# The product of attention and V moves on PE from the end of a step to its start, directly behind the scores

## The chip, the cores and the metric

The kernel runs on one core of a Trainium2 chip. The metric is device time in microseconds of the whole program, the median of several runs. A profiled execution has a time of its own, which is given beside the runs.

Engines are named as the profile names them: PE multiplies matrices (PEld is its weight load), DVE works on vectors, ACT applies functions and copies, POOL works on vectors too, SP issues most DMAs. Each engine runs its instructions in the order of the program and waits at semaphores for the others.

## The reference, cut to what matters

```python
# q, k, v: (8, 8, 576, 64); w_in (512, 1024), conv_w (3, 1024), w_out (1024, 512)
scores = q @ k.T / 8
kth = np.partition(scores, -32, axis=-1)[..., -32:-31]      # 32nd largest of each row
scores = np.where(scores >= kth, scores, -1e9)
attn = softmax(scores)
x = (attn @ v)                                              # heads side by side: (8, 576, 512)
h = np.maximum(x @ w_in, 0)
conv = conv_w[0] * h[s-1] + conv_w[1] * h[s] + conv_w[2] * h[s+1]
out = (h * sigmoid(conv)) @ w_out
```

So for each of 64 heads: scores of 576 by 576, the 32nd largest of each row as a threshold, a softmax over what reaches it, the product with v. Then, for each of 8 batches, a gated feed-forward network over 576 rows. All of it is in 32-bit floats.

## The kernel before, in words

**Tiles.** Two heads are worked on together (a pair of heads, `pc`). A tile (`t`) is 128 rows of scores by 576 keys; two tiles, `h` = 0 and `h` = 1, make a unit. There are 288 tiles, so 144 units. Where the last 64 rows of the heads are worked on, one unit serves two products of 64 columns (`single`); otherwise a unit has one product of 128 columns (`st`).

**The loop.** `iteration(it)` issues one step for all engines. Several tiles are under way, each at another stage: in step `it` the scores of tile `it + 3` are computed (L233, for both tiles of a unit at once, in the step of the first), tile `it + 2` is copied from PSUM (`evacuate`, L243), `it` and `it - 1` go through DVE's search for the largest values, `it - 2` gets its signs (`sides`, L295), `it - 3` its exponential (`expo`, L305), `it - 4` its select and its weighing (`select` L314, `weigh` L319; this gives `e`), and `it - 5` is transposed by PE (`transposes`, L335) and copied by ACT (`transposed`, L344). Between these the feed-forward network of an earlier batch is worked on as filler: `run_units` issues matmuls of `Expand` (L451) and `Contract` (L608) by a credit that grows by a fixed amount in each step (`FEED`, `LEAN`, `EARLY`).

**Two kinds of step.** The tile whose scores come next has `h` = 0 in every second step; this step is called `crowded` in the code, and here step A. In step A the tile transposed has `h` = 0 as well, and the scores of a whole unit stand at the step's end. In the other step, B, the transposed tile has `h` = 1, and behind the filler PE issues the transposes of the reciprocals of the sums (`norms`, L395, in some steps), of the tails (the 64 keys beyond 512 of both tiles, `tails`, L353), the edges of the next scores (`edge_product`, L221 and L225), and the product with v (`av`, L374 and L377).

**The product.** When a unit's second tile has been transposed, its products are put into `av_next` with `st.at = it + 1`. The next step is crowded, so the condition keeps them, and they are issued one step later, in step B, as the last thing on PE. Their result is copied in the step after that by `av_out` (L384).

**PSUM.** One bank, `mixed`, holds the edges, the tails' transpose and the two results of products, 128 columns each. Another tile of two banks, `weights_ps`, holds the exponential, the tanh of the filler, and constants that `select` reads. Accesses of different engines to one bank are put in the order of the program by semaphores, also where they go to different columns.

**Orders.** PE, ACT, DVE and POOL take their instructions in the order in which the code issues them, in all steps of the main loop; behind it, for the rest of the filler, the order comes from the framework's scheduler. ACT's order in a step is: copies of finished filler, `sides`, `evacuate`, `transposed`, `tailed`, `av_out`, later `expo`, `edges`, `tanh`, and the copy of the reciprocals in `norms`, which goes on by DMA to the rows that POOL normalises with (`normalise`, L419 to L421).

Of the kernel before, what the change touches and what calls it, by code (L numbers as in the profile page):

```python
# [71 lines left out]
def attend_and_feed(ctx: ExitStack, tc: tile.TileContext, q, k, v, weights, out, shared, finish=None):  # L72
# [155 lines left out]
    def scores(t):  # L228
        if t.h:
            return  # L230
        if not t.edged:
            edge_product(t)
        for one in (t, t.mate) if t.single else (t,):  # L233
            kx, qx, at = one.pc.nat["k"], one.pc.nat["q"], one.st.c
            for h in range(2):
                d, keys = slice(h * D, (h + 1) * D), slice(h * TAIL, h * TAIL + MAIN)
                if t.single:
                    r = slice(half_of(one, h) * D, (half_of(one, h) + 1) * D)
                    nc.tensor.matmul(s_ps[one.h][r], lhsT=qx[d, at:at + TAIL], rhs=kx[d, keys], start=True, stop=True)
                else:  # L240
                    nc.tensor.matmul(s_ps[h], lhsT=qx[d, at:at + P], rhs=kx[d, keys], start=True, stop=True)  # L241

    def evacuate(t):  # L243
        t.row = rows[:, t.n % XBUFS]
        x = t.x = t.row[:, 8:S + 8]
        at = TAIL if t.h else 0
        nc.scalar.copy(out=x[:, at:at + MAIN], in_=s_ps[t.h])  # L247
        if t.h == 0:
            r = t.n % XBUFS
            if r + 1 < XBUFS:  # L250
                first, step = r * (S + 16) + 8 + MAIN, S + 16 - MAIN
                ends = flat[:, first:first + 2 * step].rearrange("p (h c) -> p h c", h=2)[:, :, 0:TAIL]
                nc.scalar.copy(out=ends, in_=edge_ps.rearrange("p (h c) -> p h c", h=2))
            else:
                nc.scalar.copy(out=x[:, MAIN:S], in_=edge_ps[:, 0:TAIL])
                nc.scalar.copy(out=rows[:, 0, 8:8 + TAIL], in_=edge_ps[:, TAIL:2 * TAIL])
# [78 lines left out]
    def transposes(t):  # L335
        if t.h == 0:
            t.unit.pT = att.tile([P, 2, NI, P], F32, name="pT", bufs=PTB)
            t.unit.pTt = att.tile([P, P], F32, name="pTt", bufs=PTB)
        o = TAIL if t.h else 0
        tp = t.tp = bank("pt")  # L340
        for i in range(NI):
            nc.tensor.transpose(tp[:, i * P:(i + 1) * P], t.e[:, o + i * P:o + (i + 1) * P], ident)  # L342

    def transposed(t):  # L344
        pT, tp = t.unit.pT, t.tp
        if t.single:
            nc.scalar.copy(out=pT[:, :, :, t.h * TAIL:(t.h + 1) * TAIL].rearrange("p h i c -> p i h c"),
                           in_=tp.rearrange("p (i h c) -> p i h c", i=NI, h=2))
        else:
            nc.scalar.copy(out=pT[:, t.h], in_=tp.rearrange("p (i c) -> p i c", i=NI))  # L350
# [15 lines left out]
    def av(st):  # L366
        state.avs += 1
        a = st.a = x_ps[state.avs % 2]
        c = slice(st.off, st.off + st.w)
        for i in range(NI + 1):  # L370
            for h in range(2):
                r = slice(h * D, (h + 1) * D)
                if i < NI:
                    nc.tensor.matmul(a[r, 0:st.w], lhsT=st.pc.vn[:, h, i], rhs=st.unit.pT[:, st.half[h], i, c],  # L374
                                     start=(i == 0), stop=False)
                else:
                    nc.tensor.matmul(a[r, 0:st.w], lhsT=st.pc.vt[:, h], rhs=st.unit.pTt[:, c],  # L377
                                     start=False, stop=True)

    def av_out(st):  # L380
        pc = st.pc
        if st.c == 0:
            pc.xt = att.tile([P, pc.c1 - pc.c0], F32, name=f"xt{pc.part}", bufs=3 + pc.part)
        nc.scalar.copy(out=pc.xt[:, st.c:st.c + st.w], in_=st.a[:, 0:st.w])  # L384
# [312 lines left out]
    for b in range(B):  # L697
        for part, blocks in enumerate(PARTS):
            for g in range(NPAIR):
# [3 lines left out]
                for i in blocks:  # L703
                    st = Box()
# [88 lines left out]
    av_next, out_next, rec_next, norm_wait, tail_next = [], [], [], [], []  # L793

    def iteration(it):
# [4 lines left out]
        tX, tD, tE = tiles.get(it - 3), tiles.get(it - 4), tiles.get(it - 5)  # L800
# [5 lines left out]
        while split_next() and it > NT + 4:  # L806
            pass
        crowded = n < NT and work[n].h == 0
        avs = [st for st in av_next if not crowded or it > st.at]
        av_next = [st for st in av_next if st not in avs]  # L810
        both = tE is not None and tE.h == 1
        if tE is not None:
            transposes(tE)
        if n < NT:
# [7 lines left out]
            sides(tC)  # L822
        if pre is not None:
            evacuate(pre)
        if tE is not None:
            transposed(tE)
        while tail_next:
            tailed(tail_next.pop())
        outs, out_next = out_next, []
        for st in outs:  # L830
            av_out(st)
            if st.final and st.pc.g % 2:
                norm_wait.append((it + NORM_LAG, st.pc))

        if exact:
            a_ops, b_ops = [], list(exact_ops(tB)) if tB is not None else []
# [56 lines left out]
            edge_product(work[n + 1])  # L893
        if n < NT:
            scores(tiles[n])
        for st in avs:
            av(st)
        if tE is not None and tE.k == 0:
            load_v(tE.pc)
        out_next.extend(avs)  # L900
# [21 lines left out]
    with tc.manual_schedule(engines=engines) if engines else nullcontext():  # L922
        fetch(pcs[0])
        state.fetched = 1
        load_blocks(W_FIRST)
        for it in range(-3, NT + 6):
            iteration(it)
    if finish is not None:
        finish(edge_ps[0:1, 0:1])
    while expands or contracts or any(x.waiting for x in lanes) or pool_tasks or tanh_next or tanh_now or gates:  # L930
        it += 1
        iteration(it)
# [127 lines left out]
```

## Time and profile before

| | us |
|---|---|
| median of 3 runs | 1108.52 |
| lowest and highest run | 1107.27 to 1109.16 |
| profiled execution, its own time | 1109.58 |
| span of its instructions | 1107.7 |

The granted clock of PE was 0.98 of full speed over the span and 1.00 from 200 to 1000 us. The profile's page gives busy times; a wait is the idle time of an engine before an instruction, with what ended it. The chain that ended last is followed back from the last instruction: at each step to what released it, or else to the instruction before it on the same engine. A row of the timeline has start, duration, engine, line of the code, operation, tiles and shapes, and in brackets the idle time before it with what ended it; a row of the chain has start, duration, engine, tile, line.

### The profile page before, as it was taken

The numbers are of one execution on the slowest core, as the hardware profiler recorded it, in microseconds if no ns is written. First come the engines' busy times: TensorE is split into PE (matmuls) and PEld (weight loads), VectorE is DVE, ScalarE is ACT, GpSimd is POOL, SyncE is SP. The second block draws the span as 40 slices with busy tenths as digits, with TensorE's granted clock in tenths as the row PEclk, the third lists the DMA queues.
The fourth block names the chain that finished last, engine by engine and source line by source line (L and its number), as shares of the span: only waits on it lengthen the run. The fifth ranks groups of instructions, "written<-read, shape, count | busy, mean of one in ns | idle before, by whom it ended". The sixth has DMA issues, their size and how long they took to land.

```text
span 1107.7 us, 27589 instructions
## 1 busy us (share of the span) xinstructions
PE 1021.4 (92%) x7890; PEld 762.3 (69%) x7890; DVE 1038.6 (94%) x5792; ACT 958.7 (87%) x2417; POOL 935.2 (84%) x1224
## 2 busy tenths in 40 slices
PE   6776788899999999999999999999999999998996
PEld 2443466676777777776777767776777767776985
DVE  8999999999999999999999999999999999999670
ACT  7888889989999998989999998999999998999551
POOL 6778779799989989899988989899988989899610
PEclk9979899999999999999999999999999999999998
DMA  8232212223311322212311322222311322221101
GB/s 297 88 117 65 76 53 64 68 66 96 93 45 58 118 64 72 88 57 91 107 43 48 127 66 62 81 71 92 89 62 49 99 93 63 70 62 47 37 20 42
DMA packets 71154, 85.95 MB, mean 78 GB/s; under 512 B 12848, under 2 KB 45904, under 8 KB 70992
## 3 DMA queue, kind: packets, MB, share of 16 engines
q1 hardware_dynamic: 70992, 84.09, 24.2%
q8 instruction: 65, 1.06, 0.4%
q14 instruction: 97, 0.79, 0.2%
HBM read 74.47 MB, written 9.58 MB: 76 GB/s over the span
## 4 chain that ended last, share of the span: by engine, by line
PE 55%; DVE 33%; ACT 9%; issue 1%; DMA 1%; POOL 0%; SPq 0%; ACTq 0%; POOLq 0%
PE mc L608 13%; PE me L451 12%; DVE cand L263 9%; PE pt L342 8%; PE mixed L374 8%; DVE e L330 7%; PE s L241 7%; DVE z L312 5%; DVE cand L285 3%; ACT weights_ps L309 2%; ACT side L297 2%; DVE g L520 2%; DVE rows L283 2%; PE mixed L377 2%; DVE scratch L161 2%; PE weights_ps L608 2%
## 5 line engine op out<-in xcount | busy, mean ns | idle before, releaser
L263 DVE MAX8 cand<-rows 128x8 f32<-128x82 f32 (+1 forms) x2016 | 480.6, 240 | 0.0
L302 POOL TENSOR_TENSOR z<-rows,side 128x579 f32<-128x579 f32 x288 | 347.7, 1207 | 72.0 <-ACT side L297 70.7
L309 ACT ACTIVATE weights_ps<-rows,z 128x576 f32<-128x576 f32 x288 | 220.0, 764 | 23.5 <-DVE e L330 8.2
L330 DVE SCALAR_TENSOR_TENSOR e<-rows,kth,weights_ps 128x576 f32<-128x576 f32 x288 | 231.5, 804 | 0.6 <-DVE cand L263 0.3
L451 PE MATMUL me<-x_hi,wi 128*128 128x258 f32 (+1 forms) x952 | 228.0, 310 | 0.0
L342 PEld LDWEIGHTS pt<-ident,e 128*128 128x128 f32 x1152 | 124.3, 144 | 146.3 <-issue 25.2
L297 ACT ACTIVATE side<-rows 128x576 bf16<-128x576 f32 x288 | 223.6, 776 | 0.0
L312 DVE MAX8 z<-z 128x8 f32<-128x576 f32 x288 | 213.8, 742 | 0.0
L342 PE MATMUL pt<-ident,e 128*128 128x128 f32 x1152 | 193.6, 292 | 12.3 <-DVE e L330 10.9
L608 PE MATMUL mc<-wo,split 128*128 128x512 f32 x732 | 200.0, 404 | 0.0
L350 ACT COPY pT<-pt 128x512 f32<-128x512 f32 x256 | 152.9, 597 | 42.0 <-PE pt L342 41.2
L247 ACT COPY rows<-s 128x512 f32<-128x512 f32 x288 | 166.8, 579 | 6.6 <-PE s L241 4.9
L241 PE MATMUL s<-k,q 64*128 64x512 f32 x512 | 166.2, 665 | 4.5 <-ACT rows L247 4.1
L374 PE MATMUL mixed<-pT,vn 128*64 128x128 f32 (+1 forms) x2560 | 168.3, 277 | 0.0
L451 PEld LDWEIGHTS me<-x_hi,wi 128*128 128x128 f32 x952 | 162.3, 190 | 0.2 <-ACT g L465 0.2
L374 PEld LDWEIGHTS mixed<-pT,vn 128*64 128x64 f32 x2560 | 133.4, 142 | 17.5 <-issue 1.4
L608 PEld LDWEIGHTS mc<-wo,split 128*128 128x128 f32 x732 | 128.5, 189 | 20.5
L451 PE MATMUL me<-x_lo,wi 128*128 128x258 f32 (+1 forms) x476 | 142.2, 299 | 0.0
L484 POOL TENSOR_SCALAR t<-g,cr 128x256 f32<-128x256 f32 (+1 forms) x228 | 116.5, 511 | 0.0
L283 DVE MAX8 rows<-cand 128x8 f32<-128x21 f32 x576 | 106.0, 184 | 0.0
L498 POOL TENSOR_TENSOR t<-t,t 128x256 f32<-128x256 f32 (+1 forms) x114 | 91.3, 801 | 9.5
L451 PEld LDWEIGHTS me<-x_lo,wi 128*128 128x128 f32 x476 | 91.1, 191 | 0.0
(126 smaller groups left out, 1703.0 us busy)
## 6 DMA issues: line engine op xcount, KB each, us to landing
vn<-in_v_main_dram SPq DMA_DIRECT2D x64, 256.0 KB
k<-in_k_dram SPq DMA_DIRECT2D x32, 384.0 KB
k<-in_k_dram SPq DMA_DIRECT2D x32, 352.0 KB
out_dram<-o SPq DMA_DIRECT2D x26, 256.0 KB
q<-in_q_dram SPq DMA_DIRECT2D x32, 192.0 KB
rb<-row SPq DMA_DIRECT2D x64, 96.0 KB
q<-in_q_dram SPq DMA_DIRECT2D x32, 160.0 KB
raw<-in_w_in_dram SPq DMA_DIRECT2D x16, 256.0 KB
```

What stands on the lines that cost most here:

```text
L241: nc.tensor.matmul(s_ps[h], lhsT=qx[d, at:at + P], rhs=kx[d, keys], start=True, stop=True)
L247: nc.scalar.copy(out=x[:, at:at + MAIN], in_=s_ps[t.h])
L263: yield lambda c=c, at=at, n=n: nc.vector.max(out=t.cand[:, c:8 * CHUNKS:CHUNKS], in_=t.x[:, at:at + n])
L297: nc.scalar.activation(out=t.side[:, 2:S + 2], in_=t.x, func=AF.Sign, scale=-OVER, bias=t.row[:, 7:8], accum_out=t.cnt)
L302: nc.gpsimd.tensor_tensor(t.z[:, 8:S + 11], t.row[:, 6:S + 9], t.side, ALU.mult)
L309: nc.scalar.activation(out=e_ps, in_=t.x, func=AF.Exp, scale=scale, bias=t.shift)
L312: nc.vector.max(out=t.z[:, 0:8], in_=t.z[:, 10:S + 10])
L330: nc.vector.scalar_tensor_tensor(out=t.e, in0=t.x, scalar=kth[:, t.n:t.n + 1], in1=e_ps, op0=ALU.is_ge, op1=ALU.mult, accum_out=t.pc.sums[ ...
L342: nc.tensor.transpose(tp[:, i * P:(i + 1) * P], t.e[:, o + i * P:o + (i + 1) * P], ident)
L374: nc.tensor.matmul(a[r, 0:st.w], lhsT=st.pc.vn[:, h, i], rhs=st.unit.pT[:, st.half[h], i, c], start=(i == 0), stop=False)
L451: nc.tensor.matmul(mm[:, 0:w], lhsT=wt, rhs=xx, start=(n == 0), stop=(n == len(ops) - 1))
L608: nc.tensor.matmul(mm[0:m], lhsT=x[:, i], rhs=wo[:, e, f], start=start, stop=stop)
```

## The change

The product is issued at the start of step B, ahead of the transposes, and no longer at its end; its condition now keeps it for one step in every case. On PE it thus stands directly behind the scores, which end step A. On ACT the copy of the transposes, `transposed`, comes behind the copies of tails and of the product before, no longer ahead of them. Filler and its credit are as they were.

```diff
         crowded = n < NT and work[n].h == 0
-        avs = [st for st in av_next if not crowded or it > st.at]
+        avs = [st for st in av_next if it > st.at]
         av_next = [st for st in av_next if st not in avs]
         both = tE is not None and tE.h == 1
+        for st in avs:
+            av(st)
         if tE is not None:
             transposes(tE)
...
         if pre is not None:
             evacuate(pre)
-        if tE is not None:
-            transposed(tE)
         while tail_next:
             tailed(tail_next.pop())
         outs, out_next = out_next, []
...
                 norm_wait.append((it + NORM_LAG, st.pc))
+        if tE is not None:
+            transposed(tE)
...
         if n < NT:
             scores(tiles[n])
-        for st in avs:
-            av(st)
         if tE is not None and tE.k == 0:
             load_v(tE.pc)
         out_next.extend(avs)
```

## Rows read from the trace of the kernel before

**Rows 1.** The page: the chain that ended last by engine; and busy time of each engine from 200 to 1000 us (stretch, length, then busy us with the number of instructions for PE, PEld, DVE, ACT and POOL, granted clock, DMA share, GB/s).

```profile
PE 55%; DVE 33%; ACT 9%; issue 1%; DMA 1%; POOL 0%; SPq 0%; ACTq 0%; POOLq 0%
...
200.00:1000.00 800.00, 777.47 (x6245) 585.63 (x6245) 779.44 (x4497) 733.33 (x1855) 735.23 (x948) 1.00 0.24 75
```

**Rows 2.** The waits of the whole span: who waited for whom, us in total, times, longest us.

```profile
ACT pT L350 <- PE pt L342: 41.2, 52, 2.2
PE mixed L353 <- ACT rows L253: 34.1, 34, 1.7
...
DVE hot L316 <- ACT weights_ps L512: 15.9, 38, 0.7
...
PE s L395 <- ACT rows L247: 13.4, 14, 1.9
...
ACT rT L397 <- PE s L395: 5.0, 11, 0.8
```

**Rows 3.** The chain that ended last: the first of seven places where it leaves PE at the reciprocals' transpose (its copy on ACT), one of them in full length from 744 to 752 us, and the last.

```profile
244.68 0.26 ACT rT L397
...
744.27 1.06 PE s L241 x4
745.33 0.59 PE pt L342 x4
...
747.78 0.12 PE s L395
...
747.92 0.03 ACT rT L397
...
750.12 0.57 ACT pT L350
...
750.85 0.16 ACT xt L384
...
751.68 0.54 ACT weights_ps L512
...
752.25 0.24 DVE hot L316 x2
...
999.57 0.03 ACT rT L397
```

**Rows 4.** The timeline of PE at the end of a step B: the product with the first four key blocks of 128, and the transposes of the next step A.

```profile
748.15 1.09 PE L374 MATMUL mixed<-pT,vn 128*64 128x128 f32 x16
...
749.39 0.66 PE L342 MATMUL pt<-ident,e 128*128 128x128 f32 x4
```

**Rows 5.** The chain that ended last: the first of three places where it leaves PE at the end of the scores (their copy on ACT), one with what follows up to the select, and the last.

```profile
313.14 0.59 ACT rows L247
...
564.75 0.59 ACT rows L247
...
565.39 0.61 ACT pT L350
...
571.02 0.23 DVE hot L316 x2
...
816.39 0.59 ACT rows L247
```

**Rows 6.** The chain that ended last, at the first and the last of four places where it comes to PE at the tails' transpose in a pair of steps without filler in step B; between them one such place, in the timeline of PE (the row with shapes) and on the chain (T0 behind it).

```profile
216.15 0.33 PE mixed L353
...
592.92 0.33 PE L353 MATMUL mixed<-ident,e 128*128 128x128 f32 x1 [0.90 <-ACT rows L253]
...
594.72 0.59 PE pt L342 x4
...
844.57 0.33 PE mixed L353
```

**Rows 7.** The chain that ended last, at the first and the last of six places where it comes to PE at the tails' transpose behind a step A without filler; between them one such place in the timelines of PE and ACT, from 644 to 651 us.

```profile
271.93 0.33 PE mixed L353
...
644.86 0.57 ACT L350 COPY pT<-pt 128x512 f32<-128x512 f32 x1
645.00 1.12 PE L241 MATMUL s<-k,q 64*128 64x512 f32 x2 [0.57 <-ACT rows L247]
645.34 0.85 ACT L364 COPY pTt<-mixed 64x64 f32<-64x64 f32 x4
646.06 0.66 PE L342 MATMUL pt<-ident,e 128*128 128x128 f32 x4
646.20 0.27 ACT L384 COPY xt<-mixed 128x128 f32<-128x128 f32 x1
...
648.69 0.33 PE L353 MATMUL mixed<-ident,e 128*128 128x128 f32 x1 [0.53 <-ACT rows L253]
...
649.17 0.69 PE L374 MATMUL mixed<-pT,vn 128*64 128x64 f32 x16
...
650.49 0.66 PE L342 MATMUL pt<-ident,e 128*128 128x128 f32 x4
...
900.34 0.33 PE mixed L353
```

**Rows 8.** The chain that ended last: where it comes to PE for the last time, from POOL, and its last row.

```profile
1023.88 0.80 PE s L451 x2
...
1099.11 0.59 ACT rows L624
```

## The prediction, made before the changed kernel was run

> **What bounds the kernel now.** I read the page first. PE and DVE are busy almost equally, ACT and POOL not far behind; in the steady 800 us PE idles 22.5 us and DVE 20.6 us [rows 1]. So no engine alone is the bound. The second view, the list of waits, shows how they hold each other up [rows 2]: PE waits for ACT before the transpose of the tails (34.1 us) and before that of the reciprocals (13.4 us); ACT waits for the transposes before it copies them (41.2 us); DVE waits for ACT's tanh before the select (15.9 us). When which of these counts, only the third view shows, the chain that ended last. Between 216 and 1004 us it passes ten times from PE by way of ACT to DVE, which I call an exit, and ten times from DVE by way of ACT back to PE, an entry. Only what changes on this chain changes the time, so I price the edit at these twenty places.
>
> A pair is two steps of the loop. Step A transposes the first tile of a unit (T0 below) and ends with the scores; step B transposes the second (T1), then come filler, sometimes reciprocals, tails, edges, and last the product. The new order on PE: scores, product, T1, filler, reciprocals, tails, edges, T0, filler, scores.
>
> **What moves and what it weighs.** The product is 20 matmuls. From its start to that of the transposes behind it 1.24 us pass (748.15 to 749.39) [rows 4]; two products of 64 columns take 1.32 us (649.17 to 650.49) [rows 7]. Nothing is added or removed, and no DMA moves: the loads of V keep their place on SP's queue. How the product runs next to its new neighbours (scores ahead, T1 behind; edges next to T0) the trace doesn't show. In the old order T1 follows the scores, and T0 the product, without a hole on PE [rows 3, 4], so I take 0. Bounds: a hole more or less of 0.05 us (a guess of a little under the overlap at such a seam) in each pair in which PE carries the chain. PE has 55% of it [rows 1], 609 us, less the 75 us of its end [rows 8], at some 7 us a pair (144 pairs in about 1020 us): 76 pairs, 3.8 us either way.
>
> **Exits.** Seven leave PE at the reciprocals' transpose. The printed one: scores, T1 at 745.33, filler, the transpose at 747.78, its copy on ACT at 747.92, and then ACT without a pause to the tanh of 751.68, for which the select waits until 752.25 [rows 3]. The product will stand between scores and T1, ahead of that transpose, so each of these exits comes 1.24 us later. The copy is in ACT's queue ahead of the next tile's sides, score copy, exponential and tanh, and they are all late with it. That tails and old product are now copied before T0's transposes changes nothing here: they follow at once on T0's copy (750.12; old product at 750.85), and in any order the sum is the same. Three more exits leave at the end of the scores: score copy at 564.75, T1's copy at 565.39, ACT to the select at 571.02 [rows 5]. Score copy and edge copy are short, so T1's copy now has product and T1 in front of it: 1.24 us later again. Exits: 10 x 1.24 = +12.4 us.
>
> **Entries.** Four run: edge copy, tails at 592.92 after 0.90 us of idle PE, edges, product, T0 at 594.72 [rows 6]. PE has done the product before, so it drops out of this piece and T0 comes 1.24 us earlier (the idle time of the pairs before gives the rest of the lead). -4 x 1.24 = -5.0 us. Six are of another kind [rows 7]: the last step A holds no filler, and the second half of the scores waits 0.57 us for its bank, until 645.00. This wait stays. Product (1.32) and T1 follow it. From T1 (646.06) to the tails (648.69) there are 2.63 us, 0.53 of them idle. New: 646.06 + 1.32 + 2.10 = 649.48 for the tails, + 0.48 for tails and edges (648.69 to 649.17) = 649.96 for T0, against 650.49: 0.53 us earlier, not 1.32. -6 x 0.53 = -3.2 us.
>
> **Sum.** +12.4 - 5.0 - 3.2 = +4.2 us. Put otherwise: a stretch of PE that is entered at the tails and left behind T1 holds as many products as before; one that is entered at the scores holds one more.
>
> **Costs taken as nothing.** The edge copy reads the bank of tails, edges and products. That an access waits for another engine's on other columns of the bank is in the rows: the tails wait for the edge copy (34.1 us), the select for the tanh (15.9 us) [rows 2], though their columns are disjoint. So the edge copy, now behind the product in the program, has to wait for it, and with it all that ACT holds behind it. I take 0, since T1's copy, next in ACT's queue, waits for T1 behind the product anyway; without that cover it would be at most the 1.24 us priced at the exits, not both. Conversely the product now waits at its new place for the copies of tails and old product. At the narrow entry they would start where T0's copy did (644.86) and take 0.85 + 0.27, to 645.98, against the product's earliest start at 646.06 [rows 7]. So the scores hide them, closely: 0 taken, and as the upper bound 0.53 at each of the six, their whole gain.
>
> The Trainium skill, PSUM — Partial Sum Buffer, section PSUM bank collisions raise a hardware error, says that accesses of two engines to one bank and quadrant must be kept apart by semaphores, even on different columns. The waits above agree, and the sum is the same without the page.
>
> **The ends.** Before 216 us DVE carries the chain, and nothing of the edit lies on it. For the last four units the product keeps its place on PE (the end of one step is the start of the next); only its copy comes a step later. A step B is 4.1 us (745.33 to 749.39). The chain enters PE for the last time from POOL at 1023.88 and then stays there to 1099.11 [rows 8]. Other filler covers the later copy: 0, at most 4.1 if the cover is gone.
>
> **Base.** The profiled execution took 1109.58 us, 1.06 more than the median of the runs (1108.52). 1109.58 + 4.2 = 1113.8; less 1.06 for the median: 1112.7.
>
> **Rivals.**
> 1. Faster: PE fills its waits with the product (47.5 us before tails and reciprocals [rows 2]), and ACT bears the later T1. For it: ACT idles 41.2 us before copies of transposes, and step A gets lighter for it. Against it: at the exits ACT makes no pause between the reciprocals and the tanh [rows 3]. It decides if ACT has 1.24 us to spare between T1 and the select. Then the entries alone count: -8.2, median 1100.3. Chance 0.15. The Trainium skill, Perfetto Trace Analysis, section Optimization Strategies, advises to keep the matmul engine going where it idles for others; by that advice alone this would be the outcome, but in this chain PE has 55%, not all.
> 2. No change: the six narrow entries win the whole product as well (6 x 0.79 = 4.7 us more), if the wait for the scores' bank isn't what ends last there. Sum -0.5, median 1108.0. Against it: the wait is in the trace, and the copy that ends it hangs on DVE and ACT, not on PE [rows 7]. Chance 0.26.
> 3. Worse: the product at its new place waits for the copies of step A. From 0.53 us on at the six narrow entries their gain is gone: +7.4, median 1115.9. For it: only 0.08 us are between. Against it: nothing is late there by itself. Chance 0.13.
>
> My forecast has 0.46: 1112.7, and by itself 1110.5 to 1115 (about 2 us either way: half the seams' bound, or half a step at the end). Over all cases the range is 1104 to 1117. It leaves out most of rival 1 (0.15) and what seams or last step would put above rival 3. A difference under 0.2% (2.2 us) can't be told from none here. Faster: rival 1 and a little of rival 2, 0.17; the same: most of rival 2 and the low edge of the forecast, 0.27; slower: the rest of the forecast and rival 3, 0.56.
>
> **What would show it.** (a) T1's copy on ACT waits for T1 where it didn't; T0's copy hardly waits any more. (b) PE's wait before the tails falls from 34.1 us to under 10. (c) ACT's wait for the reciprocals' transpose grows from 5.0 us [rows 2] to 15 or more. (d) DVE's idle time in the steady part grows from 20.6 us by nearly the sum, to 24. (e) PE's wait at the scores for the score copy grows, as its lead ends there. The prediction is wrong if DVE's idle time shrinks (rival 1), if the narrow entries vanish from the chain (rival 2), or if the product has a wait for ACT of its own (rival 3); and if the last step's copies turn up on the chain, the end moves by up to 4 us.

## The result: slower by 0.6%, by other terms than the prediction's

| | us |
|---|---|
| kernel before, median of 12 runs | 1107.99 (1106.73 to 1109.16) |
| changed kernel, median of 12 runs | 1113.16 (1111.51 to 1119.16) |
| ratio, 95% interval | 1.0062 (1.0044 to 1.0081) |
| changed kernel, profiled execution | 1118.15, span 1116.4 |

1112.7 was forecast. Seven of the changed kernel's twelve times lie at 1111.5 to 1113.3, five at 1117.6 to 1119.2; its profiled execution is of the upper group. What sets the two apart turns out to be the term that the prediction did not have.

First the page of the changed kernel, the chain that ended last by engine:

```profile
PE 57%; DVE 33%; ACT 7%; issue 1%; DMA 1%; SPq 0%; POOL 0%; ACTq 0%; POOLq 0%
```

Then its windows: the steady part, and 14 us of it in two pieces (stretch, length, busy us with the number of instructions for PE, PEld, DVE, ACT, POOL, granted clock, DMA share, GB/s).

```profile
200.00:1000.00 800.00, 774.62 (x6168) 587.48 (x6168) 771.04 (x4442) 729.91 (x1832) 726.34 (x937) 0.98 0.24 75
...
522.60:529.40 6.80, 6.55 (x53) 4.93 (x54) 5.89 (x35) 5.01 (x15) 4.19 (x6) 0.50 0.28 65
515.00:522.60 7.60, 5.99 (x41) 3.27 (x41) 7.53 (x43) 6.56 (x15) 7.43 (x9) 1.00 0.03 11
```

PE has 57% of the chain, 55% before [rows 1], and DVE idles 29.0 us in the steady part, not 20.6 (800 less its busy time). And the granted clock, 1.00 before, is 0.98. The last two rows show where: for 6.8 us it is 0.50, 1.2 GHz and no longer 2.4, and PE is nearly always busy in it. In this execution there are six such stretches between 200 and 1000 us, at 270.0 and 396.3 (3.4 us each) and at 522.6, 648.9, 778.6 and 904.9 (6.8 us each). They lie at exactly the six narrow entries, the places of [rows 7] behind a step A without filler.

The waits of the changed kernel (who waited for whom, us in total, times, longest us), beside [rows 2]:

```profile
ACT rows L253 <- PE mixed L377: 25.3, 42, 1.0
ACT pT L350 <- PE pt L342: 23.9, 64, 1.0
...
PE mixed L353 <- ACT rows L253: 19.7, 22, 1.3
...
DVE hot L316 <- ACT weights_ps L309: 17.6, 34, 1.2
DVE hot L316 <- ACT weights_ps L512: 12.2, 15, 1.2
...
ACT rT L397 <- PE s L395: 6.9, 11, 1.0
...
PE s L241 <- ACT rT L397: 6.1, 8, 1.1
```

The edge copy waits for the product (25.3 us), as it had to. PE's wait before the tails has fallen from 34.1 to 19.7. ACT's wait for the transposes has shrunk from 41.2 to 23.9, its wait for the reciprocals' transpose is 6.9 for 5.0. Ahead of the scores there is now a wait of 6.1 us for the copy of the reciprocals; before it was 0.3. The chain, where it passes from engine to engine, read as in [rows 3, 5, 7]:

```profile
245.51 0.26 ACT rT L397
...
269.35 1.47 PE s L241 x2
...
315.93 0.02 ACT pT L350
...
355.48 0.24 PE mixed L377 x4
...
355.73 0.82 DVE e L330 x2
...
472.10 2.05 PE me L451 x12
...
522.85 2.07 PE s L241 x2
...
570.87 0.02 ACT pT L350
...
906.09 2.07 PE s L241 x2
...
1011.22 0.03 ACT rT L397
```

Eight of the ten exits are of the kinds that were forecast: five at the reciprocals' copy (seven were forecast), and three, at 315.93, 570.87 and (not shown) 826.87, at T1's copy, where the score copy stood before [rows 5]. The other two lead from the end of a product straight to DVE's weighing, at 355.73 and (not shown) 866.66. The six narrow entries no longer come at the tails but at the second half of the scores, which takes 2.07 us at four of them. And there are three places of a new kind, as at 472.10, where a filler matmul waits 0.80 us for a copy (the others, not shown, at 728.05 and 984.03).

### The profile page after: what moved, and what is told of

Same layout as the page of the kernel before. It is cut to its first block, busy times and chain, and to the rows that moved or that the text cites. A ratio compares the mean times of both kernels' runs of the same rounds, so it can differ in the third digit from the quotient of the medians.

```text
span 1116.4 us, 27713 instructions
## 1 busy us (share of the span) xinstructions
PE 1043.7 (93%) x7890; PEld 776.7 (70%) x7890; DVE 1039.2 (93%) x5792; ACT 964.5 (86%) x2417; POOL 935.7 (84%) x1224
## 3 DMA queue, kind: packets, MB, share of 16 engines
q8 instruction: 65, 1.06, 0.4%
## 4 chain that ended last, share of the span: by engine, by line
PE 57%; DVE 33%; ACT 7%; issue 1%; DMA 1%; SPq 0%; POOL 0%; ACTq 0%; POOLq 0%
PE me L451 13%; PE mc L608 12%; DVE cand L263 9%; PE mixed L374 9%; PE s L241 8%; PE pt L342 8%; DVE e L330 7%; DVE z L312 5%; DVE cand L285 3%; PE mixed L377 2%; ACT weights_ps L309 2%; DVE rows L283 2%; DVE g L520 2%; PE weights_ps L608 2%; DVE scratch L161 2%; PE mixed L225 1%
## 5 line engine op out<-in xcount | busy, mean ns | idle before, releaser
L374 PEld LDWEIGHTS mixed<-pT,vn 128*64 128x64 f32 x2560 | 138.3, 149 | 115.8 <-ACT pT L350 49.0
L342 PE MATMUL pt<-ident,e 128*128 128x128 f32 x1152 | 191.1, 290 | 13.5 <-DVE e L330 11.0
L241 PE MATMUL s<-k,q 64*128 64x512 f32 x512 | 191.0, 688 | 12.1 <-ACT rT L397 6.1
L350 ACT COPY pT<-pt 128x512 f32<-128x512 f32 x256 | 153.9, 601 | 24.9 <-PE pt L342 23.9
L374 PE MATMUL mixed<-pT,vn 128*64 128x128 f32 (+1 forms) x2560 | 173.8, 284 | 0.0
L342 PEld LDWEIGHTS pt<-ident,e 128*128 128x128 f32 x1152 | 131.4, 147 | 47.2 <-issue 14.5
L241 PEld LDWEIGHTS s<-k,q 64*128 64x128 f32 x512 | 52.4, 195 | 62.2 <-ACT rows L247 26.1
```

## The experiments

Each kernel was run beside the kernel before on the same chip; ratios are to that.

**The two halves of the change.** e1 is the kernel before with this edit alone, ACT's new order; e2 is the changed kernel without it.

```diff
-        if tE is not None:
-            transposed(tE)
         while tail_next:
             tailed(tail_next.pop())
...
+        if tE is not None:
+            transposed(tE)
```

> Only the order of the copies on ACT is changed (tails and old product ahead of the transposes); the product stays at the end of step B. Theory 'place' (the product ahead of T1 and of the reciprocals is what costs): within 1 us of the kernel before, 1107 to 1109, since at the exits the three copies follow at once in any order. Rival 'copies' (the new order of the copies costs): about +5 us, 1113. Rival 'clock' (PE's lower clock at the six entries without filler is the whole cost): no change, and the granted clock of 200 to 1000 us stays 1.00.

Measured: 1108.89, ratio 1.0015 (1.0006 to 1.0024). That is 1.3 us more than the kernel before, where up to 1 was expected, and within the bound of 0.2%. The trace shows where it comes from. At two of the six narrow entries, at 646.3 and 898.8 us, the granted clock was 0.50 for 3.4 us, though the product stands at its old place. ACT's new order has made a pause there that the kernel before didn't have, 0.40 us ahead of T1:

```profile
644.64 1.12 PE L241 MATMUL s<-k,q 64*128 64x512 f32 x2 [0.56 <-ACT rows L247]
646.16 1.06 PE L342 MATMUL pt<-ident,e 128*128 128x128 f32 x4 [0.40 <-ACT pT L350]
```

The start of each weighing on DVE, set against that in the kernel before, falls back by 1.2 and 1.1 us at these two places, and in total by nothing elsewhere between 200 and 1000 us. So in this execution the new order costs only what the clock costs.

> Only the product is moved ahead of T1; ACT copies in the old order. 'Place': like the whole change, 1112 to 1114 (up to 0.5 more where step A's copy of T0 waits). 'Copies': no change, 1108. 'Clock': like the whole change, with the granted clock below 1.00 at the six entries.

Measured: 1121.76 (1117.66 to 1122.60), ratio 1.0124 (1.0107 to 1.0142). Its profiled execution took 1118.71, beside 1118.15 of the changed kernel, with low clock at the same six places. By the starts of the weighings the two executions part by less than 1 us between 200 and 1000 us. So the move of the product is enough for the whole loss. That e2 is worse than the whole change in the median goes with its clock: over the whole span it was 0.956 to 0.958 in the three runs at 1121.8 to 1122.6, and 0.962 and 0.963 in the other two. Why it fell more often there wasn't settled.

**The product behind T1.** e3 issues it between T1 and the filler, e4 also the reciprocals' transpose right behind it.

```diff
-        for st in avs:
-            av(st)
         if tE is not None:
             transposes(tE)
+        for st in avs:
+            av(st)
```

> The whole change, but with the product behind T1 and no longer ahead of it: scores, T1, product, filler. 'Place': T1's copy is no longer late, so the three exits behind the scores cost nothing (3.7 us less), those by the reciprocals still 1.24 each: 1108.5 to 1110. 'Clock': the six entries idle as long as in the whole change, so 1113 as well. 'Copies': 1113.

Measured: 1133.48 (1128.88 to 1134.47), ratio 1.0234 (1.0220 to 1.0248). That is 20 to 25 us above all that was expected. Two things stand in the trace: how one kind of work on PE joins the next (a seam, measured from the start of the one to the start of the other), and a wait. First PE's timelines, of the kernel before, the changed kernel and e3 in this order:

```profile
703.83 0.66 PE L342 MATMUL pt<-ident,e 128*128 128x128 f32 x4
704.24 0.39 PE L451 MATMUL me<-x_lo,wi 128*128 128x322 f32 x1
...
706.23 0.39 PE L225 MATMUL mixed<-k,q 128*128 128x128 f32 x2
706.55 1.09 PE L374 MATMUL mixed<-pT,vn 128*64 128x128 f32 x16
...
707.79 0.65 PE L342 MATMUL pt<-ident,e 128*128 128x128 f32 x4
708.20 0.40 PE L451 MATMUL me<-x_hi,wi 128*128 128x322 f32 x1
```

```profile
706.22 0.39 PE L225 MATMUL mixed<-k,q 128*128 128x128 f32 x2
706.44 0.60 PE L342 MATMUL pt<-ident,e 128*128 128x128 f32 x4
706.79 0.39 PE L451 MATMUL me<-x_hi,wi 128*128 128x322 f32 x1
```

```profile
707.28 0.66 PE L342 MATMUL pt<-ident,e 128*128 128x128 f32 x4
707.86 1.09 PE L374 MATMUL mixed<-pT,vn 128*64 128x128 f32 x16
```

And from the waits of e3:

```profile
ACT rows L253 <- PE mixed L377: 74.2, 82, 2.2
```

Before, edges to product take 0.32 us and T0 to filler 0.41. In the changed kernel edges to T0 take 0.22 and T0, now behind edges, to filler 0.35: 0.10 + 0.06, together about 0.15 us a pair less (the product's two other seams, scores ahead and T1 behind, are as long as those they replace, 1.06 and 1.24). In e3 T1 to product takes 0.58 where T1 to filler took 0.41, so the gain is eaten up. The medians over the steady part, of some 85 to 110 places each, are 0.317, 0.411; 0.223, 0.356; and 0.586. A seam thus has a price, and the price is in which neighbour follows which: 0.15 us by the 76 pairs that the prediction counted gives an estimate of 11.4 us. The wait, 74.2 us against 25.3, is the edge copy waiting for the product without T1 between them.

> As the run before (product behind T1), and the reciprocals' transpose directly behind the product, ahead of the filler; their copy stays where it was on ACT. 'Place': an exit by the reciprocals then comes T1 + 1.24 us behind the scores where the kernel before had T1 + filler (1.4 to 2.3), so all exits are as early as before or earlier, and the entries keep their gain: faster than before, 1102 to 1107. 'Clock': 1113, since the six entries are as they were.

Measured: 1127.36 (1126.81 to 1132.25), ratio 1.0202 (1.0180 to 1.0223). That is 6 us less than e3, but 20 us above the 1102 to 1107 of theory "place", since e4 carries e3's loss with it. What the early reciprocals do by themselves is left to e6.

**The changed kernel again.**

> The changed kernel once more, beside the three that follow. Every theory: 1111 to 1119, in the two groups of times that it had; the trace of a faster execution should show fewer of the stretches with the lower granted clock than the first one.

Measured: 1112.14, 1112.53, 1118.08 and 1118.11; ratio 1.0074 (1.0054 to 1.0094). Over the whole span the granted clock parts the two groups in all sixteen runs of this kernel: 0.968 or 0.969 in the nine faster, 0.959 to 0.965 in the seven slower. The profiled execution was of the lower group, 1112.14, and so shows where. At the third narrow entry its clock stayed up. First PE's timeline there, then that of the slower execution (the rows of filler left out):

```profile
518.62 0.63 PE L342 MATMUL pt<-ident,e 128*128 128x128 f32 x4 [0.24 <-DVE e L330]
520.12 1.12 PE L241 MATMUL s<-k,q 64*128 64x512 f32 x2 [0.87 <-ACT rT L397]
521.82 1.12 PE L241 MATMUL s<-k,q 64*128 64x512 f32 x2 [0.58 <-ACT rows L247]
522.88 0.69 PE L374 MATMUL mixed<-pT,vn 128*64 128x64 f32 x16
...
524.19 0.66 PE L342 MATMUL pt<-ident,e 128*128 128x128 f32 x4
526.12 0.27 PE L353 MATMUL mixed<-ident,e 128*128 128x128 f32 x1
...
526.46 0.60 PE L342 MATMUL pt<-ident,e 128*128 128x128 f32 x4
```

```profile
519.64 0.63 PE L342 MATMUL pt<-ident,e 128*128 128x128 f32 x4 [0.24 <-DVE e L330]
521.14 1.12 PE L241 MATMUL s<-k,q 64*128 64x512 f32 x2 [0.87 <-ACT rT L397]
522.85 2.07 PE L241 MATMUL s<-k,q 64*128 64x512 f32 x2 [0.58 <-ACT rows L247]
524.85 1.12 PE L374 MATMUL mixed<-pT,vn 128*64 128x64 f32 x16
...
527.18 1.12 PE L342 MATMUL pt<-ident,e 128*128 128x128 f32 x4
530.11 0.27 PE L353 MATMUL mixed<-ident,e 128*128 128x128 f32 x1
...
530.45 0.60 PE L342 MATMUL pt<-ident,e 128*128 128x128 f32 x4
```

The same work with the same three waits (0.24, 0.87 and 0.58 us) up to the second half of the scores. From there to the next T0 it takes 4.64 us in the one and 7.60 in the other. In [rows 7] it is 5.49 (645.00 to 650.49). The other places agree: 5.5 us at all six of the kernel before, 4.6 at all three of the faster execution where the clock held. So this piece of a narrow entry is 0.85 us shorter than before while the clock holds (0.53 was forecast), and 2.11 us longer where it falls. This execution has the low clock at three of the six places (271.2, 646.7 and 773.0, together 13.6 us), the slower one at all six (34.0 us).

The Trainium skill, TensorE: Matmul & The Clock Gate, section A second HAM failure mode: psum-queue depth-cycling, describes a kernel whose matmul engine pauses briefly between groups often enough that its clock swings between the two levels. The rows agree in kind: PE makes three short pauses ahead of the fall. They also show that the same pauses don't always bring it on.

**The clock held up.** e7 keeps PE at work in these six steps by repeating work there: T0's transposes are done four times and the first half of the scores twice (T0's transposes also in a seventh step, behind 1010 us). Nothing else changes.

```diff
+    def bare():
+        return not exact and state.it >= 71 and state.it % 36 == 35 and state.it < NT
...
-        for i in range(NI):
+        for i in list(range(NI)) * (4 if bare() else 1):
...
+                    for _ in range(2 if bare() and h == 0 else 1):
```

> The changed kernel with redundant work on PE in the six steps A without filler: T0 is transposed four times and the first half of the scores computed twice, with the same results; no wait is taken away. 'Clock': the granted clock stays at 2.4 GHz there and all of the loss goes, 1107 to 1108. 'Place': only what the lower clock adds at the six entries goes (in the trace they cost 1.6 to 3.3 us each where 0.7 was worked out, so 5 to 9 us of the slower group of times, less of the faster), and the median comes to 1108 to 1111, still not under the kernel before.

Measured: 1104.02 (1103.40 to 1104.58), ratio 0.9965 (0.9952 to 0.9978). Below both expectations, and below the kernel before. The windows of e7, steady part and the 20 us around the fourth narrow entry:

```profile
200.00:1000.00 800.00, 782.67 (x6354) 597.53 (x6351) 781.97 (x4518) 740.48 (x1862) 738.75 (x951) 1.00 0.25 76
630.00:650.00 20.00, 19.61 (x176) 14.81 (x173) 19.93 (x114) 18.75 (x48) 18.17 (x23) 1.00 0.27 84
```

And PE's timeline in the latter:

```profile
640.48 1.94 PE L346 MATMUL pt<-ident,e 128*128 128x128 f32 x16 [0.24 <-DVE e L331]
642.35 2.46 PE L242 MATMUL s<-k,q 64*128 64x512 f32 x6
644.74 0.69 PE L378 MATMUL mixed<-pT,vn 128*64 128x64 f32 x16
```

The clock is 1.00 throughout, the pauses of 0.87 and 0.58 us are filled, and DVE idles 18.0 us, less than before. Is it the clock that gave this? The start of each weighing on DVE in e7 was set against that in the two executions of the changed kernel. Between 200 and 1000 us the distance grows only behind the narrow entries with low clock: in the slower execution by 1.4, 1.4, 2.8, 2.4, 2.8 and 2.4 us (13.1 together), in the faster one by 1.4, 1.4 and 2.5 us at its three, and by nothing at the three where its clock held, though e7 repeats work there too. Everywhere else the changed kernel and e7 keep step to within 0.1 us. So 3.4 us at low clock cost 1.4, and 6.8 us cost 2.4 to 2.8. (The faster execution had lost another 1.2 us at 144.9 us, behind 6.8 us of low clock, before the repeated work of e7 begins.)

The same repeated work in the kernel before is the control.

> The kernel before with the same repeated work on PE as in e7_kept_busy: in the six steps A without filler, T0's transposes four times and the first half of the scores twice. Theory 'clock': the kernel before has its full clock in these six places anyway (granted clock 1.00 from 200 to 1000 us), so the repeated work wins nothing; it adds up to 1.5 to 2 us of PE in front of T1 at six places, part of it in PE's idle time: 1108 to 1114, no faster than before. Theory 'idle PE' (repeated work helps by something other than the clock, so e7's gain doesn't belong to the change): the kernel before gains as after did, 9 to 11 us, to 1097 to 1099.

Measured: 1106.58, ratio 0.9994 (0.9984 to 1.0003): nothing. Its steady part has clock 1.00, as the kernel before has it without help:

```profile
200.00:1000.00 800.00, 783.64 (x6325) 594.86 (x6325) 779.47 (x4496) 732.72 (x1855) 735.02 (x948) 1.00 0.24 75
```

So what e7 gained is the clock that the change had lost, by the product's move (e2) and, less often, by ACT's order (e1). e7 against e9 (0.9965 against 0.9994) gives the price of the change where the clock is no issue: 0.29%, some 3 us faster.

**The reciprocals early.** e6 is the changed kernel with the reciprocals' transpose ahead of the filler, so that the new wait of the scores for its copy goes; e8 adds e7's repeated work.

```diff
+    def norms_pe(pc, tp):
+        nc.tensor.transpose(tp[0:2 * pc.n, 0:P], pc.duo.rec[:, 0:2 * pc.n], ident)
...
-        nc.tensor.transpose(tp[0:2 * n, 0:P], pc.duo.rec[:, 0:2 * n], ident)
...
             evacuate(pre)
+        for pc in () if crowded else rec_next:
+            norms_pe(pc, s_ps[0])
```

> The changed kernel with the reciprocals' transpose directly behind T1, ahead of the filler. Theory 'place': the exits by the reciprocals leave PE 1.24 + T1 behind the scores, 0.2 to 1 us earlier than in the kernel before, and the scores no longer wait for the reciprocals' copy (some 0.6 us in seven pairs): 5 to 9 us less than the changed kernel. 'Clock': no change against the changed kernel, since the six entries are as they were.

Measured: 1106.56 (1105.65 to 1110.19), ratio 0.9991 (0.9982 to 0.9999). Only two stretches of low clock are left in the steady part (271.5 and 896.2, 3.4 us each).

> Both edits together. 'Place': the two gains add up, as they lie at different places of the chain: 1099 to 1106, under the kernel before. 'Clock': as the run with redundant work alone, 1107 to 1108.

Measured: 1101.96 (1100.48 to 1103.11), ratio 0.9943 (0.9930 to 0.9955), the fastest kernel here. Against e7 the early reciprocals are worth 2 us. So most of the 7 to 9 us by which e6 lies below the changed kernel goes back to the clock.

**The edge copy.** In e10 (from e3), e11 (from the changed kernel) and e12 (from e8) ACT issues it behind T1's copy.

```diff
         nc.scalar.copy(out=x[:, at:at + MAIN], in_=s_ps[t.h])
+
+    def evacuate_edge(t):
+        x = t.x
...
             transposed(tE)
+        if pre is not None:
+            evacuate_edge(pre)
```

> e3_behind_t1 (product behind T1) with one more move: ACT issues the edge copy behind T1's copy, no longer ahead of it. Theory 'bank': e3's 74 us of waiting of the edge copy for the product held T1's copy, and all behind it on ACT, by 1.2 us in pairs where ACT or DVE carry the chain; with the edge copy behind, most of the 20 us that e3 lost against after comes back: 1112 to 1118. Theory 'seams' (e3 is slow because the product runs badly between T1 and filler, 0.05 us a pair, or because filler is later for it): nearly nothing comes back, 1128 to 1134.

> The changed kernel with the edge copy behind T1's copy on ACT. The prediction took the edge copy's wait for the product as nothing, since T1's copy waits for T1 behind the product anyway. If that holds: within 2 us of the changed kernel, 1111 to 1117, and the wait at the edge copy gone or short. If the wait does cost (25.3 us in the trace of after, what ACT could have done with it is only the edge copy itself, 0.2 us at some 100 pairs): 3 to 8 us faster.

> e8_early_and_busy (reciprocals' transpose ahead of the filler, and PE kept busy in the six steps) with the edge copy behind T1's copy. If the edge copy's wait is covered: 1100 to 1104, as e8. If it costs, 1096 to 1099.

Measured: e10 1134.94, ratio 1.0243 (1.0226 to 1.0260); e11 1122.20, ratio 1.0134 (1.0117 to 1.0151); e12 1104.87, ratio 0.9977 (0.9967 to 0.9987). None gains. e12 is 3 us over e8, both with clock 1.00 in the steady part. e11 is 7 to 9 us over the changed kernel, but its whole-span clock was 0.961 to 0.964, that of the changed kernel's upper group, and by the starts of the weighings only some 3 us of its loss against e7 lie away from the places of low clock. The waits of e10, then those of e11:

```profile
ACT rows L256 <- PE mixed L380: 43.3, 59, 1.5
```

```profile
ACT pT L353 <- PE pt L345: 56.3, 72, 2.0
...
PE mixed L356 <- ACT rows L256: 38.1, 44, 1.5
```

In e11 the edge copy no longer waits for the product; T1's copy waits 56.3 us in its stead, for T1 behind the product, and PE waits 38.1 us, not 19.7, for the later edge copy ahead of the tails. In e10 the edge copy still waits 43.3 us, now with the exponential behind it. So theory "bank" wasn't put to a clean test. But the wait had fallen from 74.2 us, and nothing came back. By the starts of the weighings, against e7 and between the narrow entries alone, where the clock was 1.00, e3 loses 12.1 us and e10 12.8. That speaks for the seams, 0.17 us a pair more than in the changed kernel, an estimate of some 13 us over 76 pairs. The rest of both losses lies at the narrow entries, where the clock fell as well: between 200 and 1000 us it was low for 13.7 us in e3 and for 34.1 us in e10. How that rest divides stays open.

## Why the total was right and the sum was not

**Exits and narrow entries: right in kind, not in what they add up to.** Exits at T1's copy came three times where forecast, those at the reciprocals' copy five times of seven. The narrow entry wins 0.85 us at full clock, 0.53 was said; that the wait for the scores' bank stays is right. Not foreseen there is the 0.87 us pause ahead of the first half of the scores, for the reciprocals' copy, which uses the same bank. What an entry and the next exit come to together can be read from e7 against e9, both at clock 1.00, by the starts of the weighings behind each exit. The four stretches of PE that are entered at the tails became 0.2 to 0.3 us shorter, where 0 was forecast (-1.24 and +1.24). The six that begin at a narrow entry became 0.1 to 0.6 us shorter, where each was to become 0.71 longer (-0.53 and +1.24). That is -2.6 us in all, not +4.2: at full clock no stretch got longer.

**Seams: the term mis-sized.** "Costs" of 0 with 3.8 us either way were taken for the product's new neighbours. Measured is 0.15 us less in each pair, by estimate -11.4 us over the same 76 pairs. The step that failed reads "without a hole on PE [rows 3, 4], so I take 0": a view without idle time doesn't say that two orders take the same time. Start-to-start distances do, and the one for T0 behind edges wasn't in the trace of before.

**Clock: the term that was missing.** +13 us in the profiled execution, +5 in the other, by the distances to e7. The six places were named and their wait was read [rows 7]; that the pauses there can halve the clock wasn't asked.

**Small waits: missing too.** The filler matmul at 472.10 and two like it wait 0.80 us each on the chain, 2.4 us together. The 6.1 us that the scores wait for the reciprocals' copy are another matter: 5.5 of them lie at the narrow entries, where the chain comes by the wait of the second half. With the sum of +4.2 and the seams the change would give -7.2 us at full clock; by e7 against e9 it gives some -3. Of the 4 us between, 2.4 are these waits; the rest stays open.

So +4.2 was forecast and +5.2 came, out of other terms: some -3 us at full clock, for which the seams are the only cause found, and +5 or +13 us by the clock. That the total came out as said is luck. The median lies in the lower of two groups only because seven of the twelve runs do, and without the fall of the clock the change would have been faster, the other way than forecast.

**The rivals.** Rival 1 (faster) fails as it stood: the chain still leaves PE by way of ACT at eight places, so ACT didn't absorb the later T1. But without the fall of the clock the change is faster, by seams that none of the rivals had. Rival 2 (no change) needs the whole product won at the narrow entries; 0.85 of 1.32 us was won at full clock, and the fall of the clock turns that round. Rival 3, a wait of the product for step A's copies, isn't on the chain; the product follows the scores without a hole.

**The marks.** (a) holds to the letter: from 200 to 1000 us ACT idles 16.8 us ahead of T1's copies and 0.0 ahead of T0's; before it was 0.0 and 35.7 (sums over the timelines of L350, some 100 copies each). (b) was too bold: 19.7 us, not under 10. (c) fails: ACT's wait for the reciprocals' transpose is 6.9 us, not 15. ACT meets the delay earlier, in the waits of edge copy and T1's copy. (d) holds in direction, 29.0 us for 24, but by the clock alone: in e7 it is 18.0, less than the 20.6 of before, which the prediction had named as a sign of being wrong. (e) holds weakly by the copy named (from 4.1 to 5.7 us), and more by one not named, that of the reciprocals (from 0.3 to 6.1).

**The edge copy's wait at nothing** holds as far as these runs go: moving the copy gained nothing in e11 and e12. The cover, T1's copy waiting for T1 anyway, is what e11 lays open, and e3, which takes T1 away from between, has three times the wait.

## What to carry over

Where one engine carries over half of the chain, price a new order of its work by the start-to-start distance of each new pair of neighbours, and bound those that the trace doesn't have by the spread of all that it has, not by a guess: 0.15 us in each of 76 pairs is by estimate more than twice the whole forecast. Ask of each place where a change makes PE pause whether the granted clock holds there; if the times of one kernel fall into two groups, set two of its executions side by side at the places of low clock. Test such a cause by keeping PE at work in those few places, with the same repeated work in the old kernel as the control.

## What was not expected of the hardware

The granted clock fell to 0.50 behind pauses of 0.24, 0.87 and 0.58 us, for 3.4 or 6.8 us, in one execution and not in another of the same kernel at the same place. In the kernel before, pauses of 0.57 and 0.53 us at the same place [rows 7] never brought it down in the profiled execution; in e1, with 0.40 us more ahead of T1, it fell at two places of six. One such stretch put off what follows by 1.1 to 1.4 us (3.4 us long) or by 2.4 to 2.8 us (6.8 us long). And repeated work that fills the pauses (in e7 transposes of 1.94 us for 0.63, scores of 2.46 for twice 1.12) took no time that could be measured, as e9 shows.
